# A retention and SwiGLU kernel: the norm's power on three columns, and two units with plain products beside the weight decoding

## The chip, the cores and the metric

The kernel runs on one core of one Trainium2 chip. The metric is the device time of one execution in microseconds (us). A core has five engines with queues of their own: TensorE (PE in the profile, its weight loads PEld), VectorE (DVE), ScalarE (ACT), GpSimd (POOL) and SyncE (SP). [...] Transfers are issued here from the queues of SP and ACT.

## The reference

Causal retention with a decay per head, then an RMS norm and a SwiGLU block:

```python
batch, n_heads, seq, head_dim = (8, 8, 576, 64)          # q, k, v in float32
scores = scale * np.matmul(q, k.transpose(0, 1, 3, 2))
gamma = 1.0 - 2.0 ** (-5.0 - np.arange(H))
ret = scores * np.where(rel >= 0, gamma ** rel, 0.0)     # rel = row - column
x = (ret @ v) as (4608 tokens, 512)                      # heads side by side
...
rms = np.sqrt(np.mean(x * x, axis=-1, keepdims=True) + 1e-06)
xn = x / rms * rms_g
g = xn @ w_gate                                          # 512 x 1536
silu = g * (1.0 / (1.0 + np.exp(-g)))
out = silu * (xn @ w_val) @ w_out                        # 1536 x 512
```

The three weight matrices come as float64. The kernel reads their 32-bit words and makes float32 of them on the chip.

## The kernel before, in words

**Attention.** There are 32 jobs: a batch and a pair of heads. `load(j)` brings q, k and v in; `prepare(j)` transposes q and k on DVE and scales v on ACT. `slot(j)` issues the products of job j (`scores`, `states`, then on DVE `weigh`) and the rest of job j-1 (`values`, `carried`, which ends with the multiplication that writes the job's part of x), then prepares job j+1 and loads job j+2.

**FFN.** The 4608 tokens are cut into 12 units of 384 columns, x stored with channels on the partitions (4 blocks of 128). For a unit, `norm_0` squares x on ACT and adds the four blocks on DVE; `norm_1` sums over the partitions by a product with ones, adds epsilon on DVE and raises to -0.5 on POOL; `norm_2` multiplies x by the result and rms_g on DVE, and forms the sums that the fast products need. `up(u, m, g)` computes a group of four feature blocks of the gate (m = 0, Silu on ACT) or the value (m = 1, multiplied into h on DVE) by a scheme of seven half products instead of eight (Strassen-Winograd), so that the weights need four combined blocks too: each `w_up[m]` has 14 slabs, in which 0 to 7 are first the weights themselves, and slabs 4, 5 and 8 to 13 later hold combinations. `join` forms these on POOL as soon as a group of four chunks is there. `down(u, s)` multiplies 128 tokens of h with w_out and stores the result.

**Weights.** They come in 36 chunks of 512 KB. For each, `exponent` (one DVE and three ACT steps), `mantissa` (three DVE steps) and `join` (one DVE step) make float32 of the words; `weights_to(n)` goes on to chunk n. The words land in parts of w_out that are not yet used, the last ones in o_all, the output buffer.

**Order.** It is written out by hand: instructions are issued in the order of the Python code. First slots 0 to 4 with two chunks each, then the norm of unit 0. Then for every unit six groups and three down products; `weights_to` is called at every step of unit 0, `behind` puts the attention slots of later units and the norm of the next unit between the groups: `norm_0` after the last group, `norm_1` after the first down product, `norm_2` after the second. So the product with ones (L298) is issued behind the first down product, the power (L301) follows on POOL, and the first product of the next unit (L336) waits for the multiplications of L307. Matmuls in float32 take two passes, so that one call is two instructions in the trace.

Of the kernel before, what the change touches and what calls it, by code (L numbers as in the profile page):

```python
# [8 lines left out]

F32 = mybir.dt.float32  # L10
U32 = mybir.dt.uint32
AF = mybir.ActivationFunctionType
ALU = mybir.AluOpType
P = 128
# [6 lines left out]
def _decay_tables(H, D):  # L21

    pairs = _gamma(H).reshape(H // 2, 2).T
    rows = np.repeat(pairs, D, axis=0)
    pos = np.arange(P)
    twice = np.concatenate([pos, pos])
    t = rows[:, :, None] ** twice / np.sqrt(D), pairs.T[None] ** -pos[:, None, None], rows ** -(pos % D)[:, None], rows**P
# [10 lines left out]
def kernel(  # L40
# [21 lines left out]
    SQ = 32  # L62
    U = 384
    HU = U // 2
    NU = NTOK // U
    NH = NF // 2
    NG = NH // 2
# [26 lines left out]
    ones = const.tile([P, P], F32, name="ones")  # L94
    mhalf = cell("mhalf", -0.5)
    least = cell("least", -896.0)
    most = cell("most", 255.0)
# [130 lines left out]
    def values(j):  # L228

        d = st[j]  # L230
        av = d["av"] = [bank(f"av_{j}_{i}") for i in range(2)]
        for c in range(NC):
            n, (blk, o) = rows_of(c), place(c)
            for e in range(2):
                r = slice(e * TAIL, e * TAIL + TAIL)
                nc.tensor.matmul(  # L236
                    av[blk][e * D : e * D + D, o : o + n],
                    lhsT=d["v"][:, c, e] if c < NFULL else d["vt"][r],
                    rhs=d["ret"][:, e, c * P : c * P + n] if c < NFULL else d["rett"][r],
                    start=(c in (0, AC)), stop=False, skip_group_check=True,  # L240
                )
# [23 lines left out]
    def slot(j):  # L265
# [6 lines left out]
        if j > 0:  # L272
            values(j - 1)
        if j < len(jobs):
            weigh(j)
        if j > 0:
            carried(j - 1)
        if j + 1 < len(jobs):
            prepare(j + 1)
        if j + 2 < len(jobs):  # L280
            load(j + 2)
# [13 lines left out]
    def norm_1(u):  # L295

        ms = bank(f"ms_{u}")
        nc.tensor.matmul(ms[:, :U], lhsT=ones, rhs=t_of[u], start=True, stop=True)  # L298
        r = t_of[u] = temp(f"r_{u}")
        nc.vector.tensor_scalar(out=r, in0=ms[:, :U], scalar1=EPS, scalar2=None, op0=ALU.add)  # L300
        nc.gpsimd.tensor_tensor(out=r, in0=r, in1=mhalf.to_broadcast([P, U]), op=ALU.pow)  # L301

    def norm_2(u):

        x = x_of[u]
        for c in range(NHP):
            nc.vector.scalar_tensor_tensor(  # L307
                out=x[:, c], in0=x[:, c], scalar=rms_g[:, c : c + 1], in1=t_of[u],
                op0=ALU.mult, op1=ALU.mult,
            )  # L310
        b11, b12 = x[:, :2, :HU], x[:, :2, HU:]
        b21, b22 = x[:, 2:, :HU], x[:, 2:, HU:]
        t = ffn.tile([P, 3, 2, HU], F32, tag="sums", name=f"sums_{u}")
        t2, t3, t4 = (t[:, i] for i in range(3))
        for o, a, b in ((t3, b22, b12), (b12, b12, b11), (t2, b22, b12), (t4, b21, t2)):
            nc.vector.tensor_tensor(out=o, in0=a, in1=b, op=ALU.subtract)

        t_of[u] = b11, b21, b12, t4, t2, t3, b22
# [5 lines left out]
    def up(u, m, g):  # L324
# [53 lines left out]
        result(f + NH, 0, "c21", u2, w)  # L378
        yield

    def down(u, s):
        ps = bank(f"out_{u}_{s}")
        for f in range(NF):
            nc.tensor.matmul(  # L384
                ps[:, :DM], lhsT=h_of[u][:, f, s * P : s * P + P], rhs=w_out[:, f],
                start=(f == 0), stop=(f == NF - 1),
            )
        o = o_all[:, (u * (U // P) + s) % 2]
# [97 lines left out]
    def join(i):  # L486
        if i in words_of:
            dst = chunks[i][0]
            nc.vector.scalar_tensor_tensor(
                out=dst, in0=dst, scalar=2.0**-20, in1=exp_of.pop(i).bitcast(F32),  # L490
                op0=ALU.mult, op1=ALU.mult,
            )
            del words_of[i]
        if i < n_up and i % 4 == 3:
            g, m = divmod(i // 4, 2)
            w = w_up[m][:, :, 2 * g * P : 2 * g * P + 2 * P]
            for o, a, b, op in (
                (S3, A11, A21, ALU.subtract), (S1, A21, A22, ALU.add),
                (S2, S1, A11, ALU.subtract), (S4, A12, S2, ALU.subtract),
            ):  # L500
                o, a, b = (w[:, 2 * n : 2 * n + 2] for n in (o, a, b))
                nc.gpsimd.tensor_tensor(out=o, in0=a, in1=b, op=op)
# [16 lines left out]

    with tc.manual_schedule():  # L520
        load(0)
        tables = zip((gq, gv, gt, gc, causal, causal_t), (*_decay_tables(H, D), *_causal_tables()))
# [6 lines left out]
        nc.vector.memset(ones, 1.0 / DM)  # L529
# [6 lines left out]
        for j in range(NHP + 1):  # L536
            slot(j)
            weights_to(2 * j)
        for part in (norm_0, norm_1, norm_2):
            part(0)  # L540
        step = 0

        def behind(u, i):
            at, n = SLOTS[u % 3]
            if i in at:
                slot(u // 3 * 8 + n + at.index(i))
            if u + 1 < NU and 5 <= i < 8:
                (norm_0, norm_1, norm_2)[i - 5](u + 1)

        for u in range(NU):  # L550
            for i in range(2 * NG):
                g, m = divmod(i, 2)
                weights_to(4 * i + 4)
                for _ in up(u, m, g):
                    step += 1
                    weights_to(8 + 2 * step // 3)
                behind(u, i)
            weights_to(len(chunks))
            for s in range(U // P):
                down(u, s)  # L560
                behind(u, 2 * NG + s)

# [26 lines left out]
```

## Time and profile before

| | us |
|---|---|
| three runs | 1874.83, 1875.89, 1876.75 |
| median | 1875.89 |
| profiled execution | 1874.94 |
| its span, first to last instruction | 1872.9 |
| TensorE busy | 1228.9 |
| POOL busy | 772.5 |
| DVE busy | 605.4 |
| ACT busy | 298.2 |

Busy time is the time in which an engine has an instruction in work; a row of a timeline gives start, duration, engine, line, operation, output and inputs, how many instructions are merged in it, and in square brackets how long the engine stood idle before it and which instruction on which engine ended that. "x" in a name stands for the tile x, after "x" at the end of a row comes the count. A row of waits gives the total in us, the number, and the longest.

### The profile page before, as it was taken

What the parts mean: (1) busy time and instruction counts of PE and PEld (TensorE: products, weight loads), DVE (VectorE), ACT (ScalarE), POOL (GpSimd) and SP (SyncE); (2) the same over time, 40 slices, a digit from 0 to 9 for tenths busy, and PEclk for the clock granted to TensorE, in tenths of its full rate; (3) what the DMA queues carried; (4) which work ended last, traced back from release to release, by engine and by line L of the source; (5) the groups of instructions that cost most, each with busy time, mean ns of one, the idle gap of its engine ahead of it and who ended that gap; (6) DMA issues with size and microseconds to landing.
All of it is one profiled execution on the core that took longest, in us unless ns stands there. A gap on an engine that the chain in (4) does not pass through costs nothing.

```text
span 1872.9 us, 17016 instructions
## 1 busy us (share of the span) xinstructions
PE 1228.9 (66%) x6968; PEld 979.0 (52%) x6968; DVE 605.4 (32%) x1185; ACT 298.2 (16%) x570; POOL 772.5 (41%) x42
## 2 busy tenths in 40 slices
PE   3207657396397399198199099199099189379199
PEld 3206553393393295194195096096097087176095
DVE  5507881141251153142152053042054054032041
ACT  3404451010021021011021022011012021011010
POOL 0492306607506604805704802902902901923900
PEclk9657878698699699599599599699599699789599
DMA  8604441001021023001022022001012010000000
GB/s 172 137 0 115 125 115 41 0 1 42 0 50 42 0 50 66 1 1 42 0 38 49 6 50 61 6 1 36 6 26 55 11 26 6 11 1 12 6 1 17
DMA packets 245310, 66.77 MB, mean 36 GB/s; under 512 B 226544, under 2 KB 238960, under 8 KB 245232
## 3 DMA queue, kind: packets, MB, share of 16 engines
q1 hardware_dynamic: 229440, 46.17, 12.0%
q10 hardware_dynamic: 15792, 19.51, 3.4%
q8 instruction: 55, 0.90, 0.2%
q14 instruction: 23, 0.19, 0.0%
HBM read 56.21 MB, written 9.44 MB: 35 GB/s over the span
## 4 chain that ended last, share of the span: by engine, by line
PE 46%; POOL 36%; DVE 9%; POOLq 3%; ACT 3%; DMA 1%; issue 1%; SPq 0%; DVEq 0%; ACTq 0%
POOL r L301 36%; PE w L336 9%; PE z L336 9%; PE x L336 9%; PE out L384 8%; PE y L336 5%; POOLq L584 3%; PE s L186 2%; PE av L236 2%; DVE x L307 1%; PE av L250 1%; DVE exp L481 1%; ACT exp L458 1%; ACT exp L457 1%; ACT exp L461 1%
## 5 line engine op out<-in xcount | busy, mean ns | idle before, releaser
L301 POOL TENSOR_TENSOR r<-r,mhalf 128x384 f32<-128x384 f32 x12 | 738.2, 61519 | 873.5 <-DVE r L300 873.5
L336 PE MATMUL x<-x,w_gate 128*128 128x192 f32 x576 | 127.1, 371 | 551.4 <-DVE x L307 537.6
L336 PEld LDWEIGHTS x<-x,w_gate 128*128 128x128 f32 x576 | 111.0, 219 | 563.0 <-issue 547.5
L384 PE MATMUL out<-w_out,h 128*128 128x512 f32 x864 | 374.9, 593 | 0.0
L384 PEld LDWEIGHTS out<-w_out,h 128*128 128x128 f32 x864 | 163.5, 190 | 198.6 <-issue 195.6
L307 DVE SCALAR_TENSOR_TENSOR x<-x,rms_g,r 128x384 f32<-128x384 f32 x48 | 26.5, 614 | 740.4 <-POOL r L301 740.4
L360 ACT COPY m<-x 128x384 f32<-128x384 f32 x72 | 34.0, 472 | 701.5 <-PE x L336 701.5
L336 PE MATMUL w<-sums,w_val 128*128 128x192 f32 x576 | 110.9, 338 | 12.1 <-DVE c L343 12.1
L336 PE MATMUL x<-x,w_val 128*128 128x192 f32 x576 | 109.5, 334 | 8.6 <-ACT m L360 8.6
L336 PE MATMUL w<-sums,w_gate 128*128 128x192 f32 x576 | 108.9, 333 | 8.2 <-DVE h L343 8.2
L336 PE MATMUL z<-x,w_val 128*128 128x192 f32 x576 | 105.9, 327 | 2.3 <-DVE u L343 2.3
L336 PEld LDWEIGHTS w<-sums,w_val 128*128 128x128 f32 x576 | 100.4, 198 | 13.2 <-DVE c L343 13.2
L336 PE MATMUL z<-x,w_gate 128*128 128x192 f32 x576 | 105.5, 326 | 0.3 <-DVE u L343 0.3
L336 PEld LDWEIGHTS w<-sums,w_gate 128*128 128x128 f32 x576 | 98.3, 195 | 9.1 <-DVE h L343 9.1
L336 PEld LDWEIGHTS x<-x,w_val 128*128 128x128 f32 x576 | 96.1, 193 | 10.8 <-ACT m L360 10.8
L336 PEld LDWEIGHTS z<-x,w_val 128*128 128x128 f32 x576 | 95.9, 191 | 2.7 <-issue 2.7
L336 PEld LDWEIGHTS z<-x,w_gate 128*128 128x128 f32 x576 | 95.6, 190 | 1.0 <-issue 1.0
L186 PE MATMUL s<-qT,kT 64*128 64x128 f32 (+1 forms) x640 | 52.2, 304 | 34.8 <-DVE kT L161 34.8
L389 ACT COPY o_all<-out 128x512 f32<-128x512 f32 x36 | 21.1, 585 | 331.6 <-PE out L384 331.6
L343 DVE TENSOR_TENSOR u<-m,y 128x384 f32<-128x384 f32 x72 | 39.9, 554 | 103.3 <-PE y L336 95.3
L355 ACT ACTIVATE h<-h 128x384 f32<-128x384 f32 x108 | 56.1, 521 | 97.5 <-DVE h L343 97.5
L343 DVE TENSOR_TENSOR h<-u,w 128x384 f32<-128x384 f32 x72 | 39.9, 554 | 90.1 <-PE w L336 90.1
(70 smaller groups left out, 1217.5 us busy)
## 6 DMA issues: line engine op xcount, KB each, us to landing
qraw<-in_q_dram SPq DMA_DIRECT2D x128, 72.0 KB, 2.4
kraw<-in_k_dram SPq DMA_DIRECT2D x128, 72.0 KB, 2.5
out_dram<-o_all SPq DMA_DIRECT2D x36, 256.0 KB, 2.0
k<-in_k_dram SPq DMA_DIRECT2D x64, 128.0 KB, 2.8
v<-in_v_dram SPq DMA_DIRECT2D x64, 128.0 KB, 2.8
w_out<-in_moe_w_gate_dram ACTq DMA_DIRECT2D x12, 512.0 KB, 4.7
w_out<-in_moe_w_val_dram ACTq DMA_DIRECT2D x12, 512.0 KB, 3.5
w_out<-in_moe_w_out_dram ACTq DMA_DIRECT2D x9, 512.0 KB, 3.5
```

The lines of the kernel that those rows point to most:

```text
L186: nc.tensor.matmul(s[:, e, ck] if c < NFULL else s[e * n : e * n + n, 2, :n], lhsT=d["kT"][r, ck], rhs=d["qT"][r, ck], start=True, stop=True,)
L236: nc.tensor.matmul(av[blk][e * D : e * D + D, o : o + n], lhsT=d["v"][:, c, e] if c < NFULL else d["vt"][r], rhs=d["ret"][:, e, c * P : c ...
L250: nc.tensor.matmul(av[blk][:, o : o + n], lhsT=sd[j % 2][:, c - 1], rhs=d["qT"][:, c * P : c * P + n], start=False, stop=(c in (AC - 1, NC ...
L301: nc.gpsimd.tensor_tensor(out=r, in0=r, in1=mhalf.to_broadcast([P, U]), op=ALU.pow)
L307: nc.vector.scalar_tensor_tensor(out=x[:, c], in0=x[:, c], scalar=rms_g[:, c : c + 1], in1=t_of[u], op0=ALU.mult, op1=ALU.mult,)
L336: nc.tensor.matmul(ps[:, i * HU : i * HU + HU], lhsT=w_up[m][:, 2 * blk + c, cut], rhs=t_of[u][blk][:, c], start=(start and i == c == 0), ...
L343: nc.vector.tensor_tensor(out=o, in0=a, in1=pairs_of(ps), op=ALU.add)
L355: nc.scalar.activation(out=o, in_=c, func=AF.Silu)
L360: nc.scalar.copy(out=s1, in_=pairs_of(x_))
L384: nc.tensor.matmul(ps[:, :DM], lhsT=h_of[u][:, f, s * P : s * P + P], rhs=w_out[:, f], start=(f == 0), stop=(f == NF - 1),)
L389: nc.scalar.copy(out=o, in_=ps[:, :DM])
L584: with tile.TileContext(nc) as tc:
```

## The change

The norm's mean is taken with the tokens on the partitions: for each 128 tokens a product of the squares (stationary) with one column of 1/512 gives one column, so that epsilon and power work on 128 x 3 instead of 128 x 384. Three scalings of an identity by these columns give a matrix with the results on diagonals, and a product with ones brings them back as 128 x 384 in a PSUM bank, which `norm_2` reads. `norm_2` now begins with that product on TensorE.

Units 0 and 1 use no fast products: `up_plain` multiplies with the weights as they come, four outputs of 384 columns to a group. The combinations (`combine`) are issued later, each group of w_gate after unit 1's gate group, those of w_val after unit 1's down products, because the h of unit 1 lies in slabs 8 to 13 of `w_up[1]`. The order of the start is written out in `start`: slots 0 to 3 with the weights ahead of the next slot's preparation, the norm of unit 0, then groups of unit 0, slots 4 to 7 and groups of unit 1 among each other, then the down products of unit 1 and unit 0, the norm of unit 2 behind the latter. The loop over units begins at 2, and calls no weights. The tables are loaded in another order.

```diff
     def norm_1(u):
         ms = bank(f"ms_{u}")
-        nc.tensor.matmul(ms[:, :U], lhsT=ones, rhs=t_of[u], start=True, stop=True)
-        r = t_of[u] = temp(f"r_{u}")
-        nc.vector.tensor_scalar(out=r, in0=ms[:, :U], scalar1=EPS, scalar2=None, op0=ALU.add)
-        nc.gpsimd.tensor_tensor(out=r, in0=r, in1=mhalf.to_broadcast([P, U]), op=ALU.pow)
+        for s in range(NS):
+            nc.tensor.matmul(
+                ms[:, s : s + 1], lhsT=t_of[u][:, s * P : s * P + P], rhs=mean_w,
+                start=True, stop=True,
+            )
+        r = tmp.tile([P, NS], F32, tag="r", name=f"r_{u}", bufs=1)
+        nc.vector.tensor_scalar(out=r, in0=ms[:, :NS], scalar1=EPS, scalar2=None, op0=ALU.add)
+        nc.gpsimd.tensor_tensor(out=r, in0=r, in1=mhalf.to_broadcast([P, NS]), op=ALU.pow)
+        t_of[u] = temp(f"diag_{u}")
+        for s in range(NS):
+            nc.vector.tensor_scalar(
+                out=t_of[u][:, s * P : s * P + P], in0=ident, scalar1=r[:, s : s + 1],
+                scalar2=None, op0=ALU.mult,
+            )
     def norm_2(u):
         x = x_of[u]
+        rb = bank(f"rb_{u}")
+        nc.tensor.matmul(rb[:, :U], lhsT=ones, rhs=t_of[u], start=True, stop=True)
         for c in range(NHP):
             nc.vector.scalar_tensor_tensor(
-                out=x[:, c], in0=x[:, c], scalar=rms_g[:, c : c + 1], in1=t_of[u],
+                out=x[:, c], in0=x[:, c], scalar=rms_g[:, c : c + 1], in1=rb[:, :U],
                 op0=ALU.mult, op1=ALU.mult,
             )
+        if u < 2:
+            return
...
+    def up_plain(u, m, g):
+        if not (m or g):
+            h_of[u] = (
+                w_up[1][:, 8:].rearrange("p b (s t) -> p (b s) t", t=U) if u
+                else ffn.tile([P, NF, U], F32, tag="h", name=f"h_{u}")
+            )
+        for half in range(2):
+            for i in (2 * g, 2 * g + 1):
+                ps = bank(f"up_{u}_{m}_{half}_{i}")
+                for c in range(NHP):
+                    nc.tensor.matmul(
+                        ps[:, :U], lhsT=w_up[m][:, 4 * half + c, i * P : i * P + P],
+                        rhs=x_of[u][:, c], start=(c == 0), stop=(c == NHP - 1),
+                    )
+                h = h_of[u][:, half * NH + i]
+                if m:
+                    nc.vector.tensor_tensor(out=h, in0=h, in1=ps[:, :U], op=ALU.mult)
+                else:
+                    nc.scalar.activation(out=h, in_=ps[:, :U], func=AF.Silu)
+                yield
...
-        if i < n_up and i % 4 == 3:          # end of join(i)
-            g, m = divmod(i // 4, 2)
+    def combine(m, g):
         w = w_up[m][:, :, 2 * g * P : 2 * g * P + 2 * P]
         ...                                  # four combinations on POOL, as before
+    def start():
+        for j in range(NHP):
+            slot(j)
+            weights_to(2 * j)
+            following(j)
+        values(NHP - 1)
+        carried(NHP - 1)
+        for part in (norm_0, norm_1, norm_2):
+            part(0)
+        step = 0
+        order = [(0, 0, 0), 4, (0, 1, 0), 5, (0, 0, 1), 6, (0, 1, 1), 7, (0, 0, 2)]
+        order += [(1, 0, 0), (1, 1, 0), (0, 1, 2)]
+        order += [(1, m, g) for g in (1, 2) for m in range(2)]
+        for what in order:
+            if not isinstance(what, tuple):
+                slot(what, rest=what > NHP)
+                following(what)
+                if what == 2 * NHP - 1:
+                    values(what)
+                    carried(what)
+                    norm_0(1)
+                    norm_1(1)
+                continue
+            u, m, g = what
+            weights_to(8 * g + 4 * m + 4)
+            for _ in up_plain(u, m, g):
+                step += 1
+                weights_to(8 + 28 * step // 40)
+            if what == (0, 0, 2):
+                norm_2(1)
+            if u and not m:
+                combine(m, g)
+        weights_to(len(chunks))
+        for u in (1, 0):
+            for s in range(NS):
+                down(u, s)
+                if u == 0:
+                    (norm_0, norm_1, norm_2)[s](2)
+            if u:
+                for g in range(NG):
+                    combine(1, g)
+                slot(8, rest=False)
+                following(8)
+        slot(9)
+        following(9)
```

`following(j)` is the end of the old `slot(j)`: `prepare(j + 1)` and `load(j + 2)`; `slot(j, rest=False)` leaves out job j-1.

More of the change, by code (lines that the diff above doesn't have):

```diff
@@ L8 @@
 from concourse._compat import with_exitstack
+from concourse.masks import make_identity
 F32 = mybir.dt.float32
@@ L28, in _decay_tables @@
     twice = np.concatenate([pos, pos])
-    t = rows[:, :, None] ** twice / np.sqrt(D), pairs.T[None] ** -pos[:, None, None], rows ** -(pos % D)[:, None], rows**P
+    t = (
+        pairs.T[None] ** -pos[:, None, None], rows ** -(pos % D)[:, None], rows**P,
+        rows[:, :, None] ** twice / np.sqrt(D),
+    )
     return [np.ascontiguousarray(x).astype(np.float32) for x in t]
@@ L64 @@
     HU = U // 2
+    NS = U // P
     NU = NTOK // U
@@ L94 @@
     ones = const.tile([P, P], F32, name="ones")
+    ident = const.tile([P, P], F32, name="ident")
+    mean_w = cell("mean_w", 1.0 / DM)
     mhalf = cell("mhalf", -0.5)
@@ L263, in carried, with slot @@
         st[j] = {}
-    def slot(j):
+    def slot(j, rest=True):
         if j > len(jobs):
@@ L271, in slot @@
             states(j)
-        if j > 0:
+        if rest and j > 0:
             values(j - 1)
@@ L275, in slot, with following @@
             weigh(j)
-        if j > 0:
+        if rest and j > 0:
             carried(j - 1)
+    def following(j):
         if j + 1 < len(jobs):
@@ L387, in down @@
             )
-        o = o_all[:, (u * (U // P) + s) % 2]
+        o = o_all[:, (u * (NS) + s) % 2]
         nc.scalar.copy(out=o, in_=ps[:, :DM])
@@ L493, in join @@
             del words_of[i]
-        if i < n_up and i % 4 == 3:
-            g, m = divmod(i // 4, 2)
[L496 to L502, printed above, removed]
+    def combine(m, g):
+        w = w_up[m][:, :, 2 * g * P : 2 * g * P + 2 * P]
+        for o, a, b, op in (
+            (S3, A11, A21, ALU.subtract), (S1, A21, A22, ALU.add),
+            (S2, S1, A11, ALU.subtract), (S4, A12, S2, ALU.subtract),
+        ):
+            o, a, b = (w[:, 2 * n : 2 * n + 2] for n in (o, a, b))
+            nc.gpsimd.tensor_tensor(out=o, in0=a, in1=b, op=op)
     def weights_to(n):
@@ L512, in weights_to, with behind @@
             n_chunks += 1
-    SLOTS = (((0, 2, 4, 5), 5), ((6,), 9), ((1, 3, 5), 10))
+    def start():
[43 more added lines that the diff above has]
+        following(9)
+    SLOTS = (((0, 2, 4, 5), 5), ((6,), 9), ((1, 3, 5), 10))
+    def behind(u, i):
+        at, n = SLOTS[u % 3]
+        if i in at:
+            j = u // 3 * 8 + n + at.index(i)
+            slot(j)
+            following(j)
+        if u + 1 < NU and 5 <= i < 8:
+            (norm_0, norm_1, norm_2)[i - 5](u + 1)
     with tc.manual_schedule():
         load(0)
-        tables = zip((gq, gv, gt, gc, causal, causal_t), (*_decay_tables(H, D), *_causal_tables()))
+        tables = zip((causal, causal_t, gv, gt, gc, gq), (*_causal_tables(), *_decay_tables(H, D)))
         for t, values_ in tables:
@@ L528 @@
             nc.gpsimd.memset(t, 0.0)
-        nc.vector.memset(ones, 1.0 / DM)
+        nc.vector.memset(ones, 1.0)
+        make_identity(nc, ident)
         load_chunks(WAHEAD)
@@ L535 @@
         mantissa(0)
[L536 to L550, printed above, removed]
-            for i in range(2 * NG):
[L552 to L556, printed above, removed]
+        start()
+        for u in range(2, NU):
+            for i in range(2 * NG):
+                for _ in up(u, i % 2, i // 2):
+                    pass
                 behind(u, i)
-            weights_to(len(chunks))
-            for s in range(U // P):
+            for s in range(NS):
                 down(u, s)
```

1 line of the change is left out of this document (added).

## The prediction

> **What bounds the kernel now.** I read the page first: the busy shares, the slices, the chain that ended last, the costliest groups.
>
> ```profile
> PE 1228.9 (66%) x6968; PEld 979.0 (52%) x6968; DVE 605.4 (32%) x1185; ACT 298.2 (16%) x570; POOL 772.5 (41%) x42
> PE   3207657396397399198199099199099189379199
> POOL 0492306607506604805704802902902901923900
> PEclk9657878698699699599599599699599699789599
> PE 46%; POOL 36%; DVE 9%; POOLq 3%; ACT 3%; DMA 1%; issue 1%; SPq 0%; DVEq 0%; ACTq 0%
> L301 POOL TENSOR_TENSOR r<-r,mhalf 128x384 f32<-128x384 f32 x12 | 738.2, 61519 | 873.5 <-DVE r L300 873.5
> L336 PE MATMUL x<-x,w_gate 128*128 128x192 f32 x576 | 127.1, 371 | 551.4 <-DVE x L307 537.6
> ```
>
> No engine is full. PE and POOL alternate: where the POOL digits are high the PE digit falls to 0 or 1, and the clock digit with it. The chain gives POOL over a third of the span, all of it the power of L301: 12 instructions of 61.5 us. TensorE pays 537.6 us for them, in front of the first product of a unit, which waits for the normalized x of L307. The list of waits has this as one row with its count; TensorE's timeline gives the single stalls and the restart behind one.
>
> ```profile
> PE x L336 <- DVE x L307: 537.6, 12, 63.0
> 144.85 2.90 PE L336 MATMUL x<-x,w_gate 128*128 128x192 f32 x8 [63.01 <-DVE x L307]
> 358.23 2.90 PE L336 MATMUL x<-x,w_gate 128*128 128x192 f32 x8 [42.41 <-DVE x L307]
> 496.37 2.90 PE L336 MATMUL x<-x,w_gate 128*128 128x192 f32 x8 [44.94 <-DVE x L307]
> 640.16 2.90 PE L336 MATMUL x<-x,w_gate 128*128 128x192 f32 x8 [42.46 <-DVE x L307]
> 643.52 2.77 PE L336 MATMUL y<-sums,w_gate 128*128 128x192 f32 x8 [0.46 <-DVE sums L316]
> 646.13 1.47 PE L336 MATMUL z<-x,w_gate 128*128 128x192 f32 x8
> 647.43 1.46 PE L336 MATMUL x<-x,w_gate 128*128 128x192 f32 x8
> 501.11 1.46 PE L336 MATMUL z<-x,w_gate 128*128 128x192 f32 x8
> ```
>
> The reader sees four of the twelve stalls (units 0 to 3). Once warm, products follow each other in 1.30 us (646.13 to 647.43); the first two after a stall take longer. From the start of x to that of z: 5.97 us at unit 3 and 4.74 at unit 2, against 2.60: a restart costs 2.1 or 3.4 us; I take 2.7. So there are two stages: a start up to unit 2 at 496.4 us, and ten like units in 1376.5 us, with nine stalls between them worth 537.6 - 63.0 - 42.4 - 44.9 = 387.3 us.
>
> **The change, part by part. 1: the norm of units 3 to 11.** Here is the present boundary, in the timelines of PE, DVE and POOL:
>
> ```profile
> 415.52 10.46 PE L384 MATMUL out<-w_out,h 128*128 128x512 f32 x24
> 425.92 1.42 PE L186 MATMUL s<-qT,kT 64*128 64x128 f32 x20
> 429.97 0.86 PE L298 MATMUL ms<-sq,ones 128*128 128x384 f32 x2
> 430.67 20.76 PE L384 MATMUL out<-w_out,h 128*128 128x512 f32 x48
> 433.38 0.52 DVE L300 TENSOR_SCALAR r<-ms 128x384 f32<-128x384 f32 x1
> 434.05 61.52 POOL L301 TENSOR_TENSOR r<-r,mhalf 128x384 f32<-128x384 f32 x1 [76.62 <-DVE r L300]
> ```
>
> Of the 61.5 us, 20.8 lie beside the second and third down products; the rest is the stall. Priced per column, the power costs 61.52/384 = 0.16 us; three columns are 0.5 us. The trace has no narrow power: a floor is those 0.5 us, a ceiling the whole 61.5. The nearest row of POOL with the same operation type is the combining of weights:
>
> ```profile
> L502 POOL TENSOR_TENSOR w_gate<-w_gate 128x512 f32<-128x512 f32 x12 | 16.3, 1360 | 84.4 <-DVE w_gate L489 83.7
> L301 POOL TENSOR_TENSOR r<-r,mhalf x12: 61515/61516/61536, 82.5 to 1718.1; 128x384 f32<-128x384 f32 x12
> L300 DVE TENSOR_SCALAR r<-ms 128x384 f32<-128x384 f32 x12 | 6.6, 548 | 47.7 <-PE ms L298 47.7
> L307 DVE SCALAR_TENSOR_TENSOR x<-x,rms_g,r 128x384 f32<-128x384 f32 x48 | 26.5, 614 | 740.4 <-POOL r L301 740.4
> L343 DVE TENSOR_TENSOR u<-m,y 128x384 f32<-128x384 f32 x72 | 39.9, 554 | 103.3 <-PE y L336 95.3
> L316 DVE TENSOR_TENSOR sums<-x 128x384 f32<-128x384 f32 x24 | 13.4, 558 | 0.8
> ```
>
> It handles 512 columns in 1.36 us, fixed part included, so what is fixed in a POOL instruction is under 1.4 us; I take 1 us for the new power, up to 1.9. The extremes of the twelve powers differ by 0.02 us: it is arithmetic, not waiting. [...] Here the first power, 82.5 us into the span, is as long as the others. [...]
>
> The new chain is: column sums (six passes of one column; weight loading sets their time, and I take the 0.7 us of today's two passes, between 0.3 and 1.2), epsilon, power, three scalings of the identity on DVE (under 0.55 us each by L300), then on TensorE the product with ones (two passes of 384, again 0.7 us, new), then four multiplications that read its bank (0.61 by L307; L343, which reads a bank too, is no slower than L316). Up to the scaled identity that is some 3.5 us. norm_1 is issued behind the first down product, norm_2 behind the second, 10.3 us later: the new product with ones finds its operand ready with some 6 us to spare. DVE then needs 4 x 0.61 + 4 x 0.56 = 4.7 us beside the third down product, 10.3 us. **Nothing is late, so the stall goes to zero**, and with it the restart. Queued behind the two new waits: on DVE, behind the scalings that wait for POOL, only the work of the same norm, or of a slot already issued; on TensorE, behind the product with ones, the third down product, which does not need it. If the power takes over some 7 us, that product is late by the excess. POOL has nothing else in this stage.
>
> Ten units: 1376.5 - 387.3 - 9 x 2.7 + 9 x 0.7 = **971 us**.
>
> **2: the start.** The powers of units 0 to 2 go, units 0 and 1 are computed as plain products, and weights are decoded beside them. What sets the pace of that decoding today:
>
> ```profile
> 242.14 0.72 ACT L457 ACTIVATE exp<-exp,least 128x512 f32<-128x512 uint32 x1 [1.33 <-DVE exp L453]
> 257.86 0.72 ACT L457 ACTIVATE exp<-exp,least 128x512 f32<-128x512 uint32 x1 [0.87 <-DVE exp L453]
> 248.33 0.69 DVE L481 SCALAR_TENSOR_TENSOR exp<-w_out,exp 128x512 uint32<-128x512 uint32 x1 [0.77 <-ACT exp L461]
> 257.74 1.22 DVE L208 TENSOR_TENSOR ret<-s,causal 128x1024 f32<-128x1024 f32 x1
> 262.23 0.38 DVE L474 TENSOR_SCALAR w_out<-o_all 128x512 uint32<-128x512 uint32 x1
> 275.51 0.43 DVE L453 TENSOR_SCALAR exp<-o_all 128x512 uint32<-128x512 uint32 x1 [2.79 <-DMA o_all<-in_moe_w_out_dram]
> ```
>
> Four chunks lie between the first two rows: 3.93 us each, DVE waiting for three ACT steps in every one, with one product's addition hidden in it. An attention slot holds DVE 4.5 us (257.74 to 262.23). Check on today's stage: 28 chunks x 3.93 + 4 x 4.5 = 128, and it took 144.9 to 279: 134. So DVE with ACT, not TensorE, paces the start. The rows of its beginning:
>
> ```profile
> 29.05 1.23 DVE L208 TENSOR_TENSOR ret<-s,causal 128x1024 f32<-128x1024 f32 x1 [4.82 <-PE av L236]
> 40.05 1.22 DVE L208 TENSOR_TENSOR ret<-s,causal 128x1024 f32<-128x1024 f32 x1
> 75.96 1.75 ACT L290 ACTIVATE sq<-x 128x384 f32<-128x384 f32 x4
> 187.75 1.49 DVE L474 TENSOR_SCALAR w_gate<-w_out 128x512 uint32<-128x512 uint32 x1
> ```
>
> *Up to the first product.* weights_to now stands before the transposes of the next slot (following), so TensorE's scores and values, 4.8 us in the row at 29.05, no longer lie beside decoding in slots 2 and 3: +9.6. Two chunks fewer come first (-7.9) and one weigh fewer (-2.3, half of the slot's 4.5). The squares of unit 0 then begin at about 75 instead of 75.96. From there to the power it took 6.5 us (to 82.5); power 1, identity 0.8, product with ones at half clock 1.3 and the first multiplication 0.6 follow: first product at **85 us**, where 144.85 stands now. The loads (SP's queue, issued by following) come one decode later, with a slot's time to land; tables in another order and the identity on POOL fall into the first 15 us, before TensorE has any work.
>
> *Decoding.* 30 chunks remain: 30 x 3.93 = 118. Slots 4 to 7: 18. Norm of unit 1, in which DVE waits for ACT, TensorE and POOL in turn: 10, and 2.5 for its multiplications. A fourth addition in each of four value groups: 2. Two of the POOL combinations of w_gate now fall beside decoding (six groups did; the row at 187.75 is one that POOL slowed, 1.49 against some 0.42): 6. The last chunks share o_all and wait for their load: 3. Sum 160: all weights at 245 us. TensorE's part beside it: a down product of 24 passes x 512 columns takes 10.3 us, so a pass of 384 takes 0.32, a plain step (4 blocks x 2 passes) 2.58, and 48 steps 124; with slots some 143. It fits in 160, with gaps, the more so as DVE is relieved of the sums and combinations of the fast products. (48 plain steps are 14 us longer than two units of 42 products at 1.30.)
>
> *After the last weight.* Five banks let TensorE run ahead of DVE and ACT; I count half of the last eight steps as not yet done: 10, so 255. Then six down products 61.8, slots 8 and 9 some 2.1 + 4.1 (425.92 to 429.97 is a full one), column sums and product with ones 1.4: unit 2 begins at **325 us** instead of 496.4. The norm of unit 2 lies beside the down products of unit 0, and its multiplications beside slot 9. Twelve combinations of w_val (16 us of POOL) wait until unit 1's down products have read the second h out of their place; the power of unit 2 queues behind them, but two down products, 20.6 us, cover them.
>
> Bounds: TensorE alone at full clock needs 143 + 61.8 + 7.6 from 85 on, 297; DVE as above with every addition unhidden and all eight last steps open, some 350.
>
> **Sum.** 325 + 971 = 1296 us of span. The profiled execution took 1874.94 us with a span of 1872.9, 2 us around it, and lies 0.05% below the median of the runs. So **1298 us**.
>
> **Rivals.** *The start lags.* If TensorE, waiting for weights in the first five groups, stays at half clock there, their 20 steps and four slots cost 70 us more than at full clock, of which some 25 to 30 fit into DVE's time: +45, 1343 us. For it: clock digits of 7 and 8 in slices 3 to 5. Against it: four steps in a row are 10 us, longer than the restart of 5 us seen above.
>
> *The power's time is fixed, not per column: slower.* Then the norms cost 61.5 us as before, but TensorE's product with ones, ahead of the third down product, waits for it: a stall of 61.5 - 7 + 2.7 for each of nine, 515 where 412 stand now with the restarts, and in the start DVE stands still twice and TensorE once: 60 + 60 + 50. 1298 + 515 + 170 = 1983 us. With F us for a power the same terms give about 1250 + 12 F: it ends slower from F = 52 on, and 20 us would give 1490. Against it: L502's 1.36 us. No row shows a narrow power.
>
> *The clock falls under unbroken load.* TensorE's stretches end after some 100 us now (unit 2 from 496.4 to the stall at 640.16 - 42.46 = 597.7). If the throttle held the mean that the cores view gives, 0.832, over the 971 us, they would take 1167: 1494 us.
>
> ```profile
> core 0: 1872.9 us, clock 0.832
> ```
>
> [...]
>
> **How the numbers follow.** Forecast 0.80, alone 1265 to 1325 (start 297 to 350, small terms); lagging start 0.09; a fixed or half-fixed power 0.03 slower and 0.04 between; clock 0.04. Low end: 297 + 971 + 2 = 1270, less 5 if restarts were the dearer kind. High end: the lagging start with the upper bound of small terms, 1355. Differences of 0.2% are about what a measurement of this kernel can tell from none; only the fully fixed power ends slower, and something between would have to hit the mark exactly to be the same: faster 0.96, same 0.01, slower 0.03.
>
> **What would show it.** Right: POOL's share of the chain gone, the power at 0.5 to 2 us; no idle time over 1 us before the first x of units 3 to 11, units some 86 us without slots; clock near 1 from unit 2 on; unit 2 at 297 to 350 us; DVE waiting for exp in the start. Wrong: TensorE waiting for the scaled identity in front of rb; x of a unit waiting for L307's successor; the plain steps at 5 us each; a granted clock below 1 in the long stage.

## The result, and the profile after

| | before | after |
|---|---|---|
| median, same chip (us) | 1876.32 | 1285.31 |
| lowest and highest of four runs after (us) | | 1284.93, 1285.90 |
| profiled span (us) | 1872.9 | 1283.3 |
| TensorE, POOL busy (us) | 1228.9, 772.5 | 1210.7, 43.5 |

The ratio of the times is 0.685, with a 95% interval of 0.684 to 0.686: 591 us less. The forecast was 1298 us, in a range of 1265 to 1355. One execution of an experiment below, first_and_light, ran at a granted clock of 0.844 in the mean, where the three others of that kernel had 0.978 to 0.982, and took 1443 us; its cause is not known, and it is left out of every comparison.

The page of the changed kernel, in the order in which that of the old one was read: busy shares, slices, the chain that ended last, and of the groups the new power, the new product with ones and the multiplications behind them.

```profile
PE 1210.7 (94%) x6752; PEld 920.5 (72%) x6752; DVE 569.3 (44%) x1154; ACT 289.8 (23%) x558; POOL 43.5 (3%) x44
PE   2359799999999999999999999999999999999998
POOL 0000011140000000000000000000000000000000
PEclk8669999999999999999999999999999999999999
PE 88%; DVE 5%; ACT 3%; DMA 2%; SPq 1%; issue 1%; ACTq 0%; POOL 0%; DVEq 0%
L314 POOL TENSOR_TENSOR r<-r,mhalf 128x3 f32<-128x3 f32 x12 | 10.2, 852 | 1038.6 <-DVE r L313 1038.6
L328 PE MATMUL rb<-diag,ones 128*128 128x384 f32 x24 | 10.5, 521 | 2.0 <-DVE diag L317 2.0
L330 DVE SCALAR_TENSOR_TENSOR x<-x,rms_g,rb 128x384 f32<-128x384 f32 x48 | 26.3, 610 | 88.6 <-PE rb L328 88.6
```

The holes in the row of PE are gone, and the clock digits with them: from the sixth slice to the last but one both stand at 9. POOL, over a third of the chain before, has 0% of it. The power takes 0.85 us where it took 61.5. TensorE works 18 us less than before in all; nearly all that was saved is idle time.

The list of TensorE's waits, whole, in us in total, times, and the longest:

```profile
PE s L193 <- DVE kT L168: 43.7, 4, 17.8
PE ms L308 <- DVE sq L301: 13.7, 2, 11.3
PE av L243 <- DVE ret L215: 4.7, 1, 4.7
PE up L418 <- DVE x L330: 2.5, 2, 1.8
PE rb L328 <- DVE diag L317: 2.0, 1, 2.0
PE x L361 <- ACT m L385: 1.5, 1, 1.5
PE av L257 <- ACT sd L231: 0.9, 1, 0.9
```

69 us in all, of which 57 are the first two rows, all but 2.4 us of them before the first product of unit 0. The row of 537.6 us has no successor: TensorE waits for the multiplications (now L330) 2.5 us, and for the scaled identity 2.0 us, once, in unit 0. How the new chain lies at a boundary, in the timelines of PE, POOL and DVE around the begin of unit 3:

```profile
393.77 0.72 PE L308 MATMUL ms<-mean_w,sq 128*128 128x1 f32 x6
394.36 10.55 PE L432 MATMUL out<-w_out,h 128*128 128x512 f32 x24
394.84 0.85 POOL L314 TENSOR_TENSOR r<-r,mhalf 128x3 f32<-128x3 f32 x1 [94.56 <-DVE r L313]
395.73 0.68 DVE L317 TENSOR_SCALAR diag<-ident,r 128x128 f32<-128x128 f32 x3 [1.03 <-POOL r L314]
404.74 0.81 PE L328 MATMUL rb<-diag,ones 128*128 128x384 f32 x2
405.38 10.46 PE L432 MATMUL out<-w_out,h 128*128 128x512 f32 x24
405.58 2.19 DVE L330 SCALAR_TENSOR_TENSOR x<-x,rms_g,rb 128x384 f32<-128x384 f32 x4 [9.18 <-PE rb L328]
409.58 0.56 DVE L341 TENSOR_TENSOR sums<-x,sums 128x384 f32<-128x384 f32 x1
415.68 1.46 PE L361 MATMUL x<-x,w_gate 128*128 128x192 f32 x8
```

The scaled identity is done at 396.41 (395.73 + 0.68), the product with ones reads it at 404.74: 8.3 us to spare. DVE has the unit's x and sums done at 410.14, TensorE wants them at 415.68 and starts without a gap, its first product at 1.46 us where it took 2.90.

The start, in TensorE's timeline:

```profile
43.31 2.49 PE L193 MATMUL s<-qT,kT 64*128 64x128 f32 x20 [10.01 <-DVE kT L168]
59.84 2.49 PE L193 MATMUL s<-qT,kT 64*128 64x128 f32 x20 [10.01 <-DVE kT L168]
86.91 13.47 PE L418 MATMUL up<-x,w_gate 128*128 128x384 f32 x32 [0.71 <-DVE x L330]
157.84 12.14 PE L418 MATMUL up<-x,w_gate 128*128 128x384 f32 x32
172.43 10.56 PE L418 MATMUL up<-x,w_gate 128*128 128x384 f32 x32 [1.80 <-DVE x L330]
244.74 31.06 PE L432 MATMUL out<-w_out,w_val 128*128 128x512 f32 x72
314.17 1.52 PE L361 MATMUL x<-x,w_gate 128*128 128x192 f32 x8
```

First product at 86.9 us, first down product at 244.7, unit 2 at 314.2. What the engines did from the first product to the down products, and from unit 2's first steps to the end (us from the start, length, then busy time and instructions of PE, PEld, DVE, ACT and POOL, granted clock, DMA share, GB/s):

```profile
84.00:244.00 160.00, 149.89 (x648) 91.86 (x649) 121.32 (x230) 80.31 (x132) 17.40 (x13) 0.95 0.50 120
330.00:1283.00 953.00, 949.73 (x5503) 757.45 (x5501) 388.78 (x791) 166.30 (x347) 7.65 (x9) 1.00 0.15 33
```

TensorE has 3 us without work in 953, at a granted clock of 1.00.

### The profile page after: what moved, and what is told of

It is laid out like the page before. It is cut to its first block, busy times and chain, and to the rows that moved or that the text cites. A ratio compares the mean times of both kernels' runs of the same rounds, so it can differ in the third digit from the quotient of the medians.

```text
span 1283.3 us, 16530 instructions
## 1 busy us (share of the span) xinstructions
PE 1210.7 (94%) x6752; PEld 920.5 (72%) x6752; DVE 569.3 (44%) x1154; ACT 289.8 (23%) x558; POOL 43.5 (3%) x44
## 3 DMA queue, kind: packets, MB, share of 16 engines
q1 hardware_dynamic: 229440, 46.17, 17.8%
## 4 chain that ended last, share of the span: by engine, by line
PE 88%; DVE 5%; ACT 3%; DMA 2%; SPq 1%; issue 1%; ACTq 0%; POOL 0%; DVEq 0%
PE out L432 29%; PE x L361 12%; PE w L361 12%; PE z L361 12%; PE up L418 7%; PE y L361 6%; PE s L193 3%; PE av L243 2%; PE av L257 2%; PE s L203 1%; ACT exp L506 1%; ACT exp L505 1%; ACT exp L509 1%; DMA vt<-in_v_dram 1%; PE rb L328 1%
## 5 line engine op out<-in xcount | busy, mean ns | idle before, releaser
L432 PE MATMUL out<-w_out,h 128*128 128x512 f32 x792 | 346.1, 594 | 0.0
L361 PE MATMUL x<-x,w_gate 128*128 128x192 f32 x480 | 88.9, 328 | 1.5 <-ACT m L385 1.5
L361 PE MATMUL x<-x,w_val 128*128 128x192 f32 x480 | 89.1, 329 | 0.0
L361 PE MATMUL z<-x,w_val 128*128 128x192 f32 x480 | 87.8, 326 | 0.0
L361 PE MATMUL w<-sums,w_val 128*128 128x192 f32 x480 | 87.8, 326 | 0.0
L361 PE MATMUL w<-sums,w_gate 128*128 128x192 f32 x480 | 87.8, 326 | 0.0
L361 PE MATMUL z<-x,w_gate 128*128 128x192 f32 x480 | 87.8, 326 | 0.0
L215 DVE TENSOR_TENSOR ret<-s,causal 128x1024 f32<-128x1024 f32 x32 | 39.1, 1223 | 108.5 <-PE av L243 76.2
L361 PEld LDWEIGHTS x<-x,w_gate 128*128 128x128 f32 x480 | 79.2, 190 | 7.1 <-issue 4.3
L193 PEld LDWEIGHTS s<-qT,kT 64*128 64x128 f32 (+1 forms) x640 | 41.0, 191 | 57.9 <-issue 35.6
L231 ACT ACTIVATE sd<-sum,gc 64x256 f32<-64x256 f32 x64 | 32.4, 506 | 214.2 <-DVE sum L225 213.5
L361 PEld LDWEIGHTS x<-x,w_val 128*128 128x128 f32 x480 | 78.8, 190 | 1.4 <-ACT m L385 1.4
L361 PEld LDWEIGHTS z<-x,w_gate 128*128 128x128 f32 x480 | 79.7, 190 | 0.0
L361 PEld LDWEIGHTS w<-sums,w_gate 128*128 128x128 f32 x480 | 79.7, 190 | 0.0
L361 PEld LDWEIGHTS w<-sums,w_val 128*128 128x128 f32 x480 | 79.7, 190 | 0.0
L361 PEld LDWEIGHTS z<-x,w_val 128*128 128x128 f32 x480 | 79.7, 190 | 0.0
L418 PE MATMUL up<-x,w_gate 128*128 128x384 f32 x192 | 67.7, 514 | 2.5 <-DVE x L330 2.5
```

The costliest lines, as they stand in the source:

```text
L193: nc.tensor.matmul(s[:, e, ck] if c < NFULL else s[e * n : e * n + n, 2, :n], lhsT=d["kT"][r, ck], rhs=d["qT"][r, ck], start=True, stop=True,)
L215: nc.vector.tensor_tensor(out=ret.rearrange("p e (c k) -> p e c k", c=NFULL), in0=s[:, :2].rearrange("p e (c k) -> p e c k", c=NFULL), in1 ...
L231: nc.scalar.activation(out=sd[j % 2][r, :, r], in_=t[r], func=AF.Copy, scale=gc[r, hp : hp + 1])
L361: nc.tensor.matmul(ps[:, i * HU : i * HU + HU], lhsT=w_up[m][:, 2 * blk + c, cut], rhs=t_of[u][blk][:, c], start=(start and i == c == 0), ...
L418: nc.tensor.matmul(ps[:, :U], lhsT=w_up[m][:, 4 * half + c, i * P : i * P + P], rhs=x_of[u][:, c], start=(c == 0), stop=(c == NHP - 1),)
L432: nc.tensor.matmul(ps[:, :DM], lhsT=h_of[u][:, f, s * P : s * P + P], rhs=w_out[:, f], start=(f == 0), stop=(f == NF - 1),)
```

## The experiments

Two theories stood after this. *Mine*: the power's 61.5 us were nearly all of it, and what the start lacks is set by decoding. *The rival*: the new start carries a large part by itself, and TensorE, not decoding, sets its length. The first four kernels divide the change and price the power, the next four look for what paces the start, the last two ask whether there is more to take there. Times in the text are medians; where two kernels were timed on different chips, the ratios to the kernel before, with their intervals, are compared.

**norm_only.** The kernel before, with the norm on three columns alone; units, order and tables as they were.

```diff
 (the kernel before)
-        nc.gpsimd.tensor_tensor(out=r, in0=r, in1=mhalf.to_broadcast([P, U]), op=ALU.pow)
+        nc.gpsimd.tensor_tensor(out=r, in0=r, in1=mhalf.to_broadcast([P, NS]), op=ALU.pow)
...      # the rest of norm_1 and norm_2 as in the change
```

> The kernel before with only the norm of three columns. If the nine stalls and the powers of units 0 to 2 are what the norm is worth: first product at 85 us instead of 144.85, units 1 and 2 some 44 and 46 us earlier, unit 2 at 346 us, then 969 as in the changed kernel: 1317 us. The new order of the start would then be worth 32 us. Rival, the plain products and the new order carry more of it: above 1340 us.

1323.18 us, a ratio of 0.7046 (0.7031 to 0.706). That is 555 of the 591 us; the new start adds some 37 (0.7046 to 0.6848 of 1877). TensorE's first product of unit 2 in the timeline, and what in the list of waits is the old start's own:

```profile
353.43 1.46 PE L354 MATMUL x<-x,w_gate 128*128 128x192 f32 x8
PE x L354 <- ACT m L378: 22.4, 5, 7.4
PE w L354 <- DVE c L361: 12.5, 3, 8.1
```

Unit 2 stands at 353.4, 39 us later than in the full change. In the old start the fast products wait for DVE's and ACT's work on their sums, and those engines decode too: 35 us in these two rows, and 8 more in a third (for h of L361). The changed kernel has 1.5 us of such waits. This fits plain products that are longer but ask less of the engines that decode; no run parts them from the new order, so their share of the 37 us is not shown.

**start_only.** The change with the power back on 384 columns.

```diff
 (the changed kernel)
-        nc.gpsimd.tensor_tensor(out=r, in0=r, in1=mhalf.to_broadcast([P, NS]), op=ALU.pow)
+        nc.gpsimd.tensor_tensor(out=r, in0=r, in1=mhalf.to_broadcast([P, U]), op=ALU.pow)
...      # the rest of norm_1 and norm_2 as in the kernel before
```

> The changed kernel with the power of 384 columns as before. Ten units as before, 1376.5 us; unit 2 at 314 + 60 + 48 + 48 = 470 us instead of 496: 1849 us. Rival, the new start by itself is worth as much as it is with the short power (32 us or more): at or below 1840 us; if plain products cost more than their order gains: above 1876.

1856.29 us, a ratio of 0.9884 (0.9864 to 0.9904): 22 us alone against 37 on top of the new norm. The list of waits says why:

```profile
PE x L347 <- DVE x L316: 435.7, 10, 48.6
PE up L404 <- DVE x L316: 115.8, 2, 63.0
```

All twelve stalls are there, the two of the plain units among them: together 551.5 us, 14 more than the 537.6 before. The rival falls: the start by itself is worth a few per cent of the saving.

**widths.** The changed kernel with a second power on POOL ahead of the real one in units 3 to 11, of 6 to 384 columns, so that one run gives the price of a column and the point from which it shows.

```diff
+    WIDTH = {3: 6, 4: 12, 5: 24, 6: 48, 7: 64, 8: 96, 9: 128, 10: 192, 11: 384}
...
+        t_of[u] = temp(f"diag_{u}")
+        n = WIDTH.get(u)
+        if n:
+            nc.gpsimd.tensor_tensor(
+                out=t_of[u][:, :n], in0=gq.rearrange("p a b -> p (a b)")[:, :n],
+                in1=mhalf.to_broadcast([P, n]), op=ALU.pow,
+            )
         nc.gpsimd.tensor_tensor(out=r, in0=r, in1=mhalf.to_broadcast([P, NS]), op=ALU.pow)
-        t_of[u] = temp(f"diag_{u}")
```

> An extra power of 6, 12, 24, 48, 64, 96, 128, 192 and 384 columns ahead of the real one of three columns, at units 3 to 11. By columns: 0.37 + 0.16 n us, so 1.3, 2.3, 4.2, 8.1, 10.6, 15.8, 20.9, 31.1 and 61.9 us; by a fixed part above 1 us the short ones would stand out. The product with ones has 8.3 us to spare, so TensorE waits for 0, 0, 0, 0, 2.3, 7.4, 12.6, 22.8 and 53.6 us, 99 in all; with four restarts of 2 us 1392 us. Rival, the third down product hides them as it does before (10.3 us more to spare): 60 us of waiting, 1350 us.

1343.51 us in its one execution, a span of 1341.4. POOL's timeline has the prices, TensorE's the stalls:

```profile
379.97 1.70 POOL L318 TENSOR_TENSOR diag<-gq,mhalf 128x6 f32<-128x6 f32 x1 [79.83 <-DVE c L375]
969.51 21.04 POOL L318 TENSOR_TENSOR diag<-gq,mhalf 128x128 f32<-128x128 f32 x1 [81.61 <-DVE c L375]
1073.41 31.23 POOL L318 TENSOR_TENSOR diag<-gq,mhalf 128x192 f32<-128x192 f32 x1 [82.04 <-DVE c L375]
1174.54 61.83 POOL L318 TENSOR_TENSOR diag<-gq,mhalf 128x384 f32<-128x384 f32 x1 [69.08 <-DVE c L375]
1106.32 1.62 PE L335 MATMUL rb<-diag,ones 128*128 128x384 f32 x2 [10.00 <-DVE diag L324]
1238.05 1.62 PE L335 MATMUL rb<-diag,ones 128*128 128x384 f32 x2 [42.98 <-DVE diag L324]
```

(61.83 - 31.23)/192 gives 0.159 us per column, and at 128 and 6 columns what is left is 0.7 us: that is the fixed part of these powers, which read a table. The kernel's own power, which reads and writes r, leaves less: 0.4 us of its 0.85 at three columns. Against the changed kernel the span grew by 58 us, of which 53 are the two idle times of 10.00 and 42.98; the product with ones behind them takes 1.62 for 0.81. My expectation of 1392 missed, because the extra power reads only a table and began when its buffer came free, some 10 to 16 us ahead of the column sums, and not behind them. So the widths from 6 to 128 columns show no stall at all. What the two stalls do show is that once the operand is late, TensorE waits the whole of its lateness in front of the product with ones: the third down product, behind it, covers nothing.

**tables.** The changed kernel with the tables loaded in the old order.

```diff
-        tables = zip((causal, causal_t, gv, gt, gc, gq), ...)
+        tables = zip((gq, gv, gt, gc, causal, causal_t), ...)
```

> The changed kernel with the tables loaded in the order of before. If the order is what brought the first scores from 15.9 to 17.8 us and the first weigh from 20.5 to 23.4 us: everything 2.5 to 3 us earlier, 1282.5 us. If the order does nothing: 1285 us.

1285.12 us, a ratio of 0.6841 (0.683 to 0.6853) beside 0.6848 (0.6837 to 0.686): no difference. The first scores came at 16.9 us here, 17.8 in the changed kernel, 18.1 in norm_only with the old order and 16.8 in start_only with the new one: that moment varies from execution to execution, whatever the order.

**following_first.** The transposes of the next slot ahead of decoding again, as in the kernel before.

```diff
             slot(j)
-            weights_to(2 * j)
             following(j)
+            weights_to(2 * j)
```

> The changed kernel with the next slot's transposes ahead of the weights in slots 0 to 3. The prediction put 9.6 us on that order: first product at 77 us instead of 86.9, all else 9.6 us earlier, 1275.7 us. Rival: scores beside decoding only move the wait to another place, 1283 us or more.

1277.26 us, a ratio of 0.6805 (0.6795 to 0.6815): 8 us better than the change (1285.31, 0.6837 to 0.686), with everything computed. In TensorE's timeline:

```profile
78.40 12.56 PE L418 MATMUL up<-x,w_gate 128*128 128x384 f32 x32 [0.71 <-DVE x L330]
236.93 31.06 PE L432 MATMUL out<-w_out,w_val 128*128 128x512 f32 x72
```

The first product comes at 78.4 instead of 86.9, the down products at 236.9 instead of 244.7. The transposes that ended the two waits of 10.01 us, quoted above, are done at 36.57 and 47.55 us here instead of 43.16 and 59.70, while the wait for the squares of unit 0 grows from 11.33 to 13.97: the first product gains 8.5 us in all, which is what the change pays for putting the weights first. It is the fastest version here that leaves nothing out.

**light_decode, half_plain, light_and_half.** Which engine paces the start? The first takes two of the three ACT steps out of every chunk (left out: the clamp at the top of the exponents). The second leaves out half of the plain products, priced at some 62 us of TensorE. The third does both.

```diff
 (light_decode)
-        nc.scalar.activation(out=e.bitcast(F32), in_=e, func=AF.Relu, bias=least)
-        nc.scalar.activation(out=e.bitcast(F32), in_=e.bitcast(F32), func=AF.Relu, bias=most, scale=-1.0)
-        nc.scalar.activation(out=e, in_=e.bitcast(F32), func=AF.Relu, bias=top, scale=-(2.0**23))
+        nc.scalar.activation(out=e, in_=e, func=AF.Relu, bias=least, scale=2.0**23)
 (half_plain, in up_plain)
-                for c in range(NHP):
+                for c in (0, NHP - 1):
```

> The changed kernel with one ACT step per chunk instead of three (the clamp of exponents above float32's range is left out; no weight of this input needs it). If decoding paces the start, as predicted, a chunk takes 2.6 to 3.2 us instead of 3.93 and the stage ends with TensorE's own 143 us after the first product, some 15 us earlier plus 4 in the slots before: 1266 us. If TensorE paces it, only its waits of 9 us and the 4 us before go: 1272 to 1276 us.

> The changed kernel with two of the four blocks in every plain product of units 0 and 1 (half of their work is left out), 62 us less for TensorE. If TensorE alone paces the start: 1285 - 62 = 1223 us, or as far as decoding lets it. If decoding is as near a bound, it ends at some 230 us instead of 238.6: 1274 us.

> Both: one ACT step per chunk and half of the plain products left out. If decoding and TensorE are each a bound close behind the other, both together give much more than the two alone: all weights at some 212 us, 1253 us. If one of them alone were the bound, this is as fast as the kernel that lightens that one.

| | time (us) | ratio to before | first product | first down product | between |
|---|---|---|---|---|---|
| the change | 1285.31 | 0.6837 to 0.686 | 86.91 | 244.74 | 157.8 |
| light_decode | 1276.76 | 0.6792 to 0.6812 | 80.77 | 236.63 | 155.9 |
| half_plain | 1276.58 | 0.6788 to 0.681 | 86.33 | 235.77 | 149.4 |
| light_and_half | 1257.63 | 0.6689 to 0.6708 | 80.15 | 216.89 | 136.7 |

The last three columns are starts in TensorE's timeline and their difference. How far single executions differ is seen in tables, whose stage is the change's own: 159.8 us (85.46 to 245.24). In the stage itself, less decoding saves 2 us, no more than two executions of the same stage differ by; less TensorE saves 8, both together 21. The medians say the same of the whole: 8.6, 8.7 and 27.7 us. light_decode missed its 1266 us and came out just above its other branch (1272 to 1276), that of TensorE as the bound. So neither engine paces the stage alone: take one away, and the other stands right behind. The rows of the windows of that stage for the three (columns as above) show the same:

```profile
81.00:237.00 156.00, 148.22 (x649) 91.40 (x650) 116.86 (x227) 41.41 (x76) 17.05 (x13) 0.95 0.51 121
86.00:236.00 150.00, 101.45 (x457) 59.82 (x458) 122.08 (x227) 80.13 (x132) 18.55 (x13) 0.83 0.50 126
80.00:217.00 137.00, 103.93 (x457) 61.19 (x458) 119.20 (x227) 40.56 (x76) 18.23 (x13) 0.82 0.57 138
```

With light decoding TensorE is busy 148 of 156 us, as in the change: it is the bound, and ACT's 41 us (80 before) buy next to nothing: DVE's waits for exp fall from 22.4 to 4.0 us, but its waits for plain products grow from 6.3 to 15.3. With half the products TensorE's busy time falls to 101 us, 48 less and not 62, as the granted clock falls with it, from 0.95 to 0.83. It is idle for a third of the stage, and DVE, with ACT in its loop, still needs nearly 150, and waits for exp to the end of them (4.8 us in seven rows from 199.66 to 229.26). The 6 us that light_decode gains otherwise lie ahead of the first product, where decoding stands in front of the slots.

**first_and_light, four_chunks.** following_first and light_decode together; and the same with only four chunks ahead of the first product instead of six, the others spread over the plain steps. In both the clamp at the top of the exponents is left out.

```diff
 (four_chunks, against first_and_light)
-            weights_to(2 * j)
+            weights_to(j + 1)
...
-                weights_to(8 + 28 * step // 40)
+                weights_to(4 + 32 * step // 40)
```

> Transposes ahead of the weights in slots 0 to 3, and one ACT step per chunk (without the clamp at the top). If the two gains lie at different places (the wait for the transposes, the wait for ACT), they add as far as the first product goes: at some 75 us, and with the 156 us that the light decoding alone had from there to the down products, 1270 us. If one hides the other: 1276 us.

> The same, with four chunks instead of six ahead of the first product, the rest spread over the steps. If TensorE now paces the start: first product 5 us earlier, 1265 us. If decoding is still as near: what the start gains, the wait before the norm of unit 1 takes back, 1270 us.

first_and_light: 1271.12 us, a ratio of 0.6768 (0.6757 to 0.6779), so the two gains add for the larger part. four_chunks: 1271.47, 0.6771 (0.676 to 0.6782): nothing more, though its first product stands at 66.7 us. The list of waits up to 240 us:

```profile
PE up L416 <- DVE w_gate L529: 6.4, 2, 5.3
PE up L416 <- DVE w_val L529: 3.1, 1, 3.1
```

TensorE now waits for weights, 9.5 us that the lists of the other kernels with the new start do not have, and the down products begin at 231.3, 164.5 us behind the first product instead of 155.9 as in light_decode. The earlier start is paid back inside the stage.

## Why the prediction was right

The sum was 1296 us of span, and the span is 1283.3. The mechanism, a stall that goes with the power's columns, came out as forecast; the error lies in one term of the start. By its own steps:

*The norm of units 3 to 11: right in all terms.* 0.85 us for a power was put at 1, within the ends of 0.5 and 61.5; some 6 us to spare for the product with ones are 8.3; DVE behind it takes 4.6 us (405.58 to 410.14) where 4.7 stood. Ten units, forecast 971 us, took 969.1 (314.17 to 1283.3). The column sums took 0.72 us where 0.7 stood, and their weight loads follow one another without a gap, five in 0.64 us (PEld, from 393.77). The step that the restart goes with the stall is shown by first products of 1.46 us. norm_only confirms the size with the old start: its ten units take 967.7 us (353.43 to 1321.1). One reading was off without consequence: of the old power's 61.5 us, 17.4 lay beside down products (434.05 to 451.43), not the 20.8 that the two products last.

*Up to the first product:* 85 forecast, 86.9 measured. The term of 9.6 us for decoding ahead of the transposes is confirmed by following_first, which gives back 8.5 of it there and 8.0 in the time.

*From there to the down products:* this is the term that was mis-sized. 160 us of decoding and 10 for the last steps were forecast, 157.8 in all were measured; those 12 us are nearly the whole error of the sum. All weights were ready at 238.6, 150 us behind the begin of decoding at 88.4, and the down products began 6.1 us later, where 10 stood: 4 of the 12 us are there. Another piece shows in DVE's timeline: the norm of unit 1 was priced at 12.5 us, as if DVE waited for ACT, TensorE and POOL in turn.

```profile
155.09 0.55 DVE L301 TENSOR_TENSOR sq<-sq,sq 128x384 f32<-128x384 f32 x1
159.21 1.67 DVE L317 TENSOR_SCALAR diag<-ident,r 128x128 f32<-128x128 f32 x3 [1.04 <-POOL r L314]
161.86 0.69 DVE L529 SCALAR_TENSOR_TENSOR exp<-w_out,exp 128x512 uint32<-128x512 uint32 x1
165.78 0.69 DVE L529 SCALAR_TENSOR_TENSOR exp<-w_out,exp 128x512 uint32<-128x512 uint32 x1 [1.23 <-ACT exp L509]
171.67 2.18 DVE L330 SCALAR_TENSOR_TENSOR x<-x,rms_g,rb 128x384 f32<-128x384 f32 x4
```

It took 5.8 us (155.09 to 160.88) and 2.2 for the multiplications, 8.0. A third is in the same rows: 161.86 to 165.78 is the cadence of 3.93 that was used for all 30 chunks, but the chunk at 161.86, right behind the norm, has no wait for ACT in it, since ACT's three steps ran while DVE was at the norm. Every slot gives DVE such a piece of other work. DVE's list of waits, from the first product to the down products, counts the chunks that do wait, 21 of 30:

```profile
DVE exp L529 <- ACT exp L509: 22.4, 21, 3.0
```

One term erred the other way: three groups of combinations, not two, fell beside decoding, and lengthened DVE's rows by more than the 6 us forecast (an estimate, in the last section). How the rest divides was not measured.

*"DVE with ACT, not TensorE, paces the start": wrong, in one direction only.* It holds for the kernel before and not for this start. TensorE's work beside decoding was put at 143 us, is 149 at a clock of 0.96 in the mean, and has 9 us of waits besides; decoding was put at 160 and is 150. So the two meet, and the stage has one length for two reasons, as light_decode and half_plain show. That the wrong bound cost the sum so little is luck: the two lengths lie close together. The forecast of DVE waiting for exp was right (the 22.4 us above) and said less than I took it to say: without two of ACT's three steps the stage was 2 us shorter.

*Down products, slots, norm of unit 2:* 70 forecast, 69.4 measured (244.74 to 314.17).

*The rivals.* The lagging start: the granted clock in the stage is 0.95 and the plain groups take 10.5 us from the second on; only the first, 13.5, and the one behind the norm of unit 1, 12.1, ran partly slow, at a granted clock of 0.78 and 0.87. So the lag is there, at some 5 us instead of 45. (The clock digits of the kernel before that spoke for it are 5, 7 and 8 in slices 3 to 5, not 7 and 8.) The fixed power: refuted by 0.85 us and by the slope in widths. What it took for granted holds: in widths, a power that came late was paid in full in front of the product with ones. Its turning point was not tested. The clock under load: 1.00 in the row from 330 us to the end, for 950 us of TensorE work on end. The first power of the changed kernel is, as in the one before, no longer than the others; POOL's timeline has it as

```profile
82.86 0.86 POOL L314 TENSOR_TENSOR r<-r,mhalf 128x3 f32<-128x3 f32 x1 [80.64 <-DVE r L313]
```

The twelve take 848 to 864 ns. It began 0.08 us after its operand was done (DVE's r, 82.62 + 0.16).

## What to carry to other kernels

Before the order of a kernel is rearranged around a long instruction, ask whether its length goes by columns: putting the tokens on the partitions made 384 columns three, and was worth 555 of 591 us, while the new start without it was worth 22. Where two chains of work, here TensorE's and that of DVE with ACT, each take nearly the whole of a stage, relieving one is worth little (2 and 8 us here) and both together far more (21): their waits name the one that is last, not how near the other is. And work that feeds another engine, as the transposes do, goes ahead of bulk work on the same queue: that exchange of two lines gave 8 us.

## What the runs showed of the hardware that was not expected

A power on POOL took 0.159 us per column of 128 float32 in widths, with a fixed part of only some 0.7 us there and 0.4 in the kernel itself; the 1.36 us of a combining of 512 columns was an upper bound two to three times too high. The multiplication that reads its operand from a PSUM bank took 610 ns (L330, the mean of 48) where the one of before, which read it from SBUF, took 614 (L307).

DVE took longer over some rows while POOL combined weights. Two rows of DVE's timeline, the same instruction ahead of and during POOL's combinations of 233.44 to 238.05:

```profile
162.47 0.69 DVE L537 SCALAR_TENSOR_TENSOR w_gate<-w_gate,exp 128x512 f32<-128x512 f32 x1
235.18 1.75 DVE L537 SCALAR_TENSOR_TENSOR w_out<-w_out,exp 128x512 f32<-128x512 f32 x1
```

1.75 us for 0.69. The excess, 1.06 us, is that of the row quoted in the prediction (1.49 for some 0.42). In the same stretch a multiplication that reads one operand from a PSUM bank (L424, at 236.85) took 0.54 us, as elsewhere. All twelve combinations of w_gate fell beside decoding, and the rows of DVE that they lengthened add up to some 9 us more than the same rows take elsewhere (an estimate from this trace; 1 us of it are the scalings at 159.21, 1.67 us for 0.68), where the prediction had 6.
